# Two layers of linear attention and gated feed-forward on one core: a broadcast through DRAM in longer rows, the feed-forward weights loaded later and in smaller pieces, and a new list of turns

## The chip, the cores and the metric

The kernel runs on one core of a Trainium2 chip. A core has five engines that run their own instruction streams in order and wait for one another by semaphores: TensorE (PE in the profile, with its weight loads as PEld), VectorE (DVE), ScalarE (ACT), GpSimd (POOL) and SyncE (SP). SyncE computes nothing here: it issues transfers (DMA). ScalarE issues some too. The metric is the device time of one execution in microseconds (us); the median of the runs shown is compared.

## The reference

The input x is 2048 rows of 512 numbers in bfloat16. Two kinds of blocks alternate, A B A B, with the same weights both times, so the kernel speaks of two layers of one A and one B each:

```
x = x + A(layernorm(x));  x = x + B(layernorm(x))      # twice

A: q, k, v = x @ wqkv                       # 32 heads of 16
   pq, pk  = q @ w_phi[h], k @ w_phi[h]     # per head, 16x16
   phi(p)  = [softmax(p), softmax(-p)]      # 32 features per head
   kv = sum over rows of phi_k^T v ;  z = sum over rows of phi_k
   out = (phi_q kv) / (phi_q z + 1e-6), heads joined, @ wo
B: h = (x @ W_gate where positive) * (x @ W_up) ;  h @ W_down      # 512 -> 1376 -> 512
```

The attention isn't causal: no query of a layer can be finished before the sums kv and z hold all 2048 keys.

## The kernel before, in words

**Tiles and slabs.** x stays in on-chip memory as 16 tiles of 128 rows (`x_sb`). Most work is done by slabs of 2, 4, 4, 4 and 2 tiles (`SLABS`); in names such as `la04` or `es/12/1` the first digit is the layer (0 or 1) and the second the slab.

**Start.** `load_x` (L732) and `load_w` (L742) bring x and the pieces of wqkv. `fold` multiplies w_phi into the key and query weights: it turns each piece by TensorE (`tr`, L713), copies it out (`evict`, L813 on VectorE, L816 on ScalarE), multiplies by a block-diagonal w_phi and copies the result to `Wkp` or `Wqp`.

**Keys.** For each slab `into_a` runs `layernorm` and then `keys`. `layernorm` takes statistics on VectorE (L840), makes the normalized row tile `ytile` on ScalarE (L882) or VectorE (L885), and turns it to `yA` (for A) or `yG` (for B): for the slabs in `XPOSE` by a transposing DMA that SyncE issues for each tile (L890), else by TensorE (L914) and copies. `keys` multiplies by `Wkp` and `wv` (all such products go through the helper `mm`, so they share L709), takes the two exponentials on ScalarE (L942), sums them by head on VectorE (L948), divides the values by these sums (`vhat`, L962, VectorE or GpSimd) and adds the products with the keys (L974) into `kvsum`.

**Queries.** After the sums of the layer, `out_of_a` takes each slab. `queries` makes the exponentials `expq` (L1043). `attend` multiplies them with the sums (L1071 and around), and from that makes `aT` (L1106): for each row and head the two factors, one for each sign of the exponential, by which `expq` has to be scaled. Head and row lie in `aT` so that they must be spread over 16 partitions each. For slabs 0 and 1 `spread` does that by TensorE (multiplied in at L1195 and L1198). For slabs 2, 3 and 4 it goes through DRAM: SyncE writes `aT` to a scratch (L1116), reads it back with each row repeated 16 times into `abT` (L1120), and `scale` (L1165) multiplies `expq` by it, one of four column groups at a time, on VectorE or GpSimd. Then come the products with `kvbd` (L1132), wo, the residual (L1202) and the normalization for B.

**Feed-forward.** `glu` does a slab's gate and up products, relu on ScalarE (L1254), gate times up on VectorE (`hT`, L1256) and the product with W_down. 1280 of the 1376 columns are in `Wg`, `Wu` and `Wd`, loaded by L761, L762 and L763; a rest of 96 goes another way with weights of its own (`Wl`, `rest`). In layer 0, `glu` of a slab is followed by the keys of layer 1 for that slab.

**Order.** The program is first recorded as a list of operations with what each reads and writes. `schedule()` then puts them in order for every engine with a cost model: among the operations that are ready it goes by `TURNS`, a list with one number for each operation. `ENG` is a table that says on which engine an operation runs or which queue issues a load, where there is a choice (`es/` for the scales, `fc` and `ft` for copies of the folded weights, `vh/` for vhat, `ot/`, `vc/`, `yc/` and `za/` for other copies out, `ld/` for loads, `ms/` for fills). `HOLD` can put operations with a tag behind a given operation on the same queue. `plan()` chooses the semaphores. The result is fixed when the kernel is built; on the chip each engine goes through its own list in order, and an instruction that waits holds up all behind it.

Of the kernel before, what the change touches and what calls it, by code (L numbers as in the profile page):

```python
# [7 lines left out]
BF16 = mybir.dt.bfloat16  # L8
# [4 lines left out]
P = 128  # L13
# [9 lines left out]
HOLD = {}  # L23
ENG = {'ap/a01/0': 'dve',
 'ap/a01/1': 'dve',
# [5 lines left out]
 'ap/a10/0': 'act',  # L31
 'ap/a11/0': 'act',
 'ap/a11/2': 'act',
 'ap/a12/3': 'act',
# [3 lines left out]
 'ap/g02/0': 'act',  # L38
 'ap/g02/1': 'act',
 'ap/g02/3': 'act',  # L40
# [5 lines left out]
 'ap/g12/1': 'act',  # L46
 'ap/g12/2': 'act',
 'ap/g13/2': 'act',
 'ap/g13/3': 'act',
# [6 lines left out]
 'em/11/02': 'act',  # L56
 'em/11/12': 'act',
 'es/02/0': 'pool',
 'es/02/1': 'pool',
 'es/02/3': 'pool',  # L60
 'es/03/3': 'pool',
 'es/04/0': 'pool',
 'es/04/2': 'pool',
 'es/12/1': 'pool',
 'es/13/0': 'pool',
 'es/13/1': 'pool',
 'es/14/0': 'pool',
 'es/14/1': 'pool',
 'es/14/2': 'pool',
 'fck1': 'act',  # L70
 'fck3': 'act',
 'ftk1': 'act',
 'ftk2': 'dve',
 'ftk3': 'act',
 'ftq1': 'dve',
 'ftq2': 'dve',
 'ld/wk1': 'act',
 'ld/wphi': 'sp',
 'ld/wq1': 'act',
 'ld/wq2': 'act',  # L80
 'ld/wv': 'act',
 'ld/x0': 'act',
 'ms/BD': 'pool',
 'ms/ZD 0': 'pool',
 'ms/hl 0': 'pool',
 'ms/kvs 0 1': 'pool',
 'ms/vsb ones': 'pool',
# [3 lines left out]
 'ot/01/1': 'dve',  # L91
 'ot/01/2': 'dve',
 'ot/02/0': 'dve',
 'ot/02/1': 'dve',
 'ot/02/2': 'dve',
 'ot/03/1': 'dve',
 'ot/03/3': 'dve',
 'ot/04/0': 'dve',
 'ot/04/2': 'dve',
 'ot/04/3': 'dve',  # L100
 'ot/10/1': 'act',
 'ot/10/2': 'dve',
 'ot/11/1': 'dve',
 'ot/11/3': 'dve',
 'ot/12/1': 'dve',
 'ot/12/3': 'dve',
 'ot/13/0': 'dve',
 'ot/13/2': 'dve',
 'ot/14/0': 'dve',
 'ot/14/3': 'dve',  # L110
# [11 lines left out]
 'rz/1/12': 'act',  # L122
 'rz/1/13': 'act',
 'rz/1/15': 'act',
 'rz/1/2': 'act',
 'rz/1/3': 'act',
 'rz/1/4': 'act',
 'rz/1/5': 'act',
 'rz/1/6': 'act',
 'rz/1/7': 'act',  # L130
 'rz/1/8': 'act',
 'rz/1/9': 'act',
 'vc/0/10': 'dve',
 'vc/0/2': 'dve',
 'vc/0/4': 'dve',
 'vc/0/5': 'dve',
 'vc/0/7': 'dve',
 'vc/0/8': 'dve',
 'vc/1/1': 'dve',
# [3 lines left out]
 'vc/1/5': 'dve',  # L143
 'vc/1/7': 'dve',
 'vc/1/9': 'dve',
 'vh/0/1/0': 'dve',
 'vh/0/10/1': 'dve',
 'vh/0/12/0': 'dve',
 'vh/0/13/0': 'dve',
 'vh/0/13/1': 'dve',  # L150
 'vh/0/14/1': 'dve',
 'vh/0/15/1': 'dve',
 'vh/0/3/1': 'dve',
 'vh/0/4/0': 'dve',
 'vh/0/4/1': 'dve',
 'vh/0/7/1': 'dve',
 'vh/1/0/1': 'dve',
 'vh/1/11/1': 'dve',
 'vh/1/12/0': 'dve',
 'vh/1/15/0': 'dve',  # L160
 'vh/1/15/1': 'dve',
 'vh/1/2/0': 'dve',
 'vh/1/2/1': 'dve',
 'vh/1/4/0': 'dve',
 'vh/1/4/1': 'dve',
 'vh/1/5/0': 'dve',
 'vh/1/6/0': 'dve',
 'vh/1/6/1': 'dve',
 'vh/1/7/1': 'dve',
 'xp/a10': 'sp',  # L170
 'xp/a14': 'sp',
 'xp/g11': 'sp',
 'yc/a00/1': 'dve',
 'yc/a01/00': 'act',
 'yc/a01/01': 'act',
 'yc/a01/02': 'act',
# [13 lines left out]
 'yc/a14/1': 'dve',  # L190
 'yc/g00/1': 'dve',
# [12 lines left out]
 'za/03': 'dve',  # L204
 'za/11': 'dve',
 'za/12': 'dve',
 'za/14': 'dve'}
# [1166 lines left out]
```

## Time and profile before

| | |
|---|---|
| median of three runs | 388.92 us (388.54 to 389.83) |
| the profiled execution's own time | 390.18 us |
| its span | 388.4 us |
| TensorE, VectorE, ScalarE, GpSimd busy | 97%, 71%, 51%, 17% of the span |
| granted clock of TensorE | 1.00 |
| moved by DMA | 27.96 MB, mean 72 GB/s |
| instruction-fetch packets of queue q8 | 29 of 16 KB |

The span is what the profile of one execution covers; its own time has some 2 us more around it. In a profile, a busy TensorE is not TensorE at its best: matmuls are pipelined, so gaps are read from the starts of successive matmuls. The span, cut by the stages of the work:

| from, to (us) | what runs | TensorE busy of the length |
|---|---|---|
| 0, 13.5 | loads, folding | 9.12 of 13.50 |
| 13.5, 30.9 | first keys, last folding | 16.29 of 17.40 |
| 30.9, 59.5 | keys of layer 0 | 27.68 of 28.60 |
| 59.5, 71.1 | sums, first queries | 10.23 of 11.60 |
| 71.1, 203 | rest of layer 0 A, feed-forward, keys of layer 1 among it | 131.68 of 131.90 |
| 203, 262 | last keys of layer 1 and first slabs of its queries | 58.81 of 59.00 |
| 262, 276 | queries of a later slab, through DRAM | 13.15 of 14.00 |
| 276, 388.4 | rest of layer 1 | 109.03 of 112.40 |

A line of a chain or of an engine's list reads: start, length (us), engine, line of the kernel, what is written and from what, how many instructions in a row. A square bracket at the end names the idle time before it and what ended it.

### The profile page before, as it was taken

How to read it: one execution, taken by the hardware profiler on the slowest of the kernel's cores; microseconds unless marked ns; L12 is line 12 of the kernel's file. 1: busy time of each engine (PE TensorE's matmuls, PEld its weight loads, DVE VectorE, ACT ScalarE, POOL GpSimd, SP SyncE). 2: the span in 40 equal slices, each digit the busy share in tenths (PEclk: the TensorE clock that was granted, in tenths of full speed). 3: DMA queues.
4: the chain of work that ended last, by engine and by line, in shares of the span. 5: the costliest groups of instructions: out<-in, count | busy, mean ns of one | idle time of the engine just before them, and what ended most of it. 6: DMA issues, size and time to landing. Idle time of an engine off the chain costs nothing.

```text
span 388.4 us, 8944 instructions
## 1 busy us (share of the span) xinstructions
PE 376.0 (97%) x3719; PEld 197.8 (51%) x3719; DVE 275.2 (71%) x560; ACT 198.6 (51%) x443; POOL 67.7 (17%) x64
## 2 busy tenths in 40 slices
PE   5999998999999999999999999999999999999996
PEld 2644454384444544444566455475444544454574
DVE  6999987978854887565986996679965556473243
ACT  3999898833542236045416689993263231334021
POOL 4044940051200200200120554001000412000000
PEclk9999999999999999999999999999999999999999
DMA  8995201043450132004004010132444121221002
GB/s 246 286 351 88 42 3 35 31 134 92 111 113 26 47 69 54 2 14 81 2 7 57 3 29 3 32 87 92 119 89 121 42 62 39 58 66 56 0 29 62
DMA packets 57545, 27.96 MB, mean 72 GB/s; under 512 B 39360, under 2 KB 55840, under 8 KB 57504
## 3 DMA queue, kind: packets, MB, share of 16 engines
q1 hardware_dynamic: 55968, 25.98, 27.0%
q10 hardware_dynamic: 1536, 1.41, 1.2%
q8 instruction: 29, 0.48, 0.5%
q14 instruction: 12, 0.10, 0.1%
HBM read 15.25 MB, written 4.00 MB: 50 GB/s over the span
## 4 chain that ended last, share of the span: by engine, by line
PE 81%; DMA 5%; DVE 5%; ACT 5%; SPq 2%; issue 1%; POOL 0%; DVEq 0%
PE pb L709 76%; PE pb L974 2%; DMA abT<-spread 2%; DMA hT<-in_A_wqkv_dram 1%; DVE expq L1198 1%; ACT expk L942 1%; SPq L1120 1%; DMA yA<-ytile 1%; PE pb L1132 1%; DVE expq L1195 1%; DVE x_sb L1202 1%; ACT hT L816 1%; PE pb L1058 1%; DMA spread<-aT 1%; PE pb L1071 1%
## 5 line engine op out<-in xcount | busy, mean ns | idle before, releaser
L709 PE MATMUL pb<-yG,Wu 128*128 128x512 bf16 (+1 forms) x400 | 94.4, 337 | 0.0
L709 PE MATMUL pb<-Wd,hT 128*128 128x512 bf16 (+4 forms) x363 | 94.2, 373 | 0.0
L709 PE MATMUL pb<-yG,Wg 128*128 128x512 bf16 (+1 forms) x400 | 92.8, 337 | 0.3 <-DVE hT L1256 0.2
L1254 ACT ACTIVATE gate_sb<-pb 128x512 bf16<-128x512 f32 x80 | 47.0, 597 | 86.3 <-PE pb L709 55.8
L1256 DVE TENSOR_TENSOR hT<-gate_sb,pb 128x512 bf16<-128x512 bf16 x80 | 54.0, 682 | 44.6 <-PE pb L709 32.3
L962 POOL TENSOR_TENSOR vhat<-vsb,rZk 128x544 bf16<-128x544 bf16 x40 | 43.2, 1102 | 110.3 <-DVE vhat L962 36.8
L1202 DVE TENSOR_TENSOR x_sb<-x_sb,pb 128x512 bf16<-128x512 bf16 x59 | 39.2, 678 | 25.1 <-PE pb L709 24.9
L709 PEld LDWEIGHTS pb<-yG,Wu 128*128 128x128 bf16 x400 | 38.9, 98 | 32.5 <-issue 0.8
L709 PEld LDWEIGHTS pb<-yG,Wg 128*128 128x128 bf16 x400 | 38.7, 98 | 31.2 <-DVE hT L1256 0.7
L709 PEld LDWEIGHTS pb<-Wd,hT 128*128 128x128 bf16 (+1 forms) x363 | 34.8, 98 | 35.9 <-issue 0.7
L1165 POOL TENSOR_TENSOR expq<-expq,abT 128x1024 bf16<-128x1024 bf16 (+1 forms) x12 | 20.5, 1720 | 140.9 <-PE pb L709 84.2
L948 DVE TENSOR_REDUCE Zk<-expk 128x64 f32<-128x1024 bf16 x32 | 38.3, 1208 | 4.4 <-ACT expk L942 4.4
L840 DVE BATCH_NORM_STATS2 stats<-x_sb 128x6 f32<-128x512 bf16 x60 | 39.7, 680 | 1.7 <-DMA x_sb<-in_A_x_dram 1.3
L709 PE MATMUL pb<-wv,yA 128*128 128x512 bf16 x128 | 38.6, 379 | 0.9 <-DMA yA<-ytile 0.9
L942 ACT ACTIVATE expk<-pb 128x512 bf16<-128x512 f32 x64 | 35.6, 611 | 6.1 <-PE pb L709 3.7
L709 PE MATMUL pb<-Wkp,yA 128*128 128x512 bf16 x128 | 38.4, 380 | 0.2 <-ACT Wkp L816 0.2
L1043 ACT ACTIVATE expq<-pb 128x512 bf16<-128x512 f32 x64 | 34.9, 615 | 1.0 <-PE pb L709 0.8
L709 PE MATMUL pb<-wo_sb,oT 128*128 128x512 bf16 x128 | 35.2, 379 | 0.0
L709 PE MATMUL pb<-yA,Wqp 128*128 128x512 bf16 (+1 forms) x160 | 33.7, 337 | 0.1
L1222 ACT ACTIVATE gate_sb<-pb 128x192 bf16<-128x192 f32 x16 | 5.3, 333 | 42.9 <-PE pb L709 42.9
L882 ACT ACTIVATE ytile<-x_sb,nmr,rstd 128x512 bf16<-128x512 bf16 x27 | 21.2, 811 | 4.4 <-DVE nmr L874 4.2
L709 PEld LDWEIGHTS pb<-yA,Wqp 128*128 128x128 bf16 x160 | 14.5, 98 | 12.3 <-issue 1.0
(94 smaller groups left out, 340.0 us busy)
## 6 DMA issues: line engine op xcount, KB each, us to landing
abT<-spread SPq DMA_DIRECT2D x32, 128.0 KB
out_dram<-x_sb SPq DMA_DIRECT2D x15, 128.0 KB, 2.7
x_sb<-in_A_x_dram SPq DMA_DIRECT2D x3, 512.0 KB
Wd<-in_B_W_down_dram SPq DMA_DIRECT2D x1, 1280.0 KB
Wg<-in_B_W_gate_dram SPq DMA_DIRECT2D x1, 1280.0 KB
Wu<-in_B_W_up_dram SPq DMA_DIRECT2D x1, 1280.0 KB
sums_scr<-abT SPq DMA_DIRECT2D x5, 256.0 KB, 2.5
Zs<-sums_scr SPq DMA_DIRECT2D x5, 256.0 KB, 2.7
```

The source lines that it names most:

```text
L709: op("pe", lambda e: e.matmul(view(ps), lhsT, rhs, start=start, stop=stop), reads=reads, writes=[ps], occ=max(25.0, 0.4167 * n + 2.6), lat ...
L840: op("dve", lambda e: e.bn_stats(stats[:, t, :], src()), reads=[res], writes=[R("st", t)], occ=580, lat=680, name=f"bn{t}")
L882: op("act", (lambda t, yb: lambda e: e.activation(ytile[:, yb, :], x_sb[:, t, :], ACT.Identity, bias=nmr[:, t, :], scale=rstd[:, t, :]))(t ...
L942: op("act", (lambda i, s, pk: lambda e: e.activation(expk[:, i, s, :], full(pk), ACT.Exp, scale=1.0 - 2.0 * s))(i, s, pk), reads=[pk], wri ...
L948: op("dve", (lambda i, zb: lambda e: e.tensor_reduce(Zk[:, zb, :], expk[:, i, :, :].rearrange("p s (h f) -> p (s h) f", f=16), AX.X, ALU.a ...
L962: op(eng, (lambda i, s, vb, rz: lambda e: e.tensor_tensor(vhat[:, i, s, :, :], vsb[:, vb, :, :], rZk[:, rz, s * 32:(s + 1) * 32].unsqueeze ...
L974: ins = e.matmul(ps.f32()[32 * i:32 * i + 32, g * 34:g * 34 + 34], expk[:, tiles[j], sg, f0:f0 + 32], vhat[:, tiles[j], sg, 8 * c + 2 * i: ...
L1043: op("act", (lambda c0, s, ps: lambda e: e.activation(eqv(st)[:, c0:c0 + per, s, :], ps.f32()[:, 0:per * n].rearrange("p (c n) -> p c n", ...
L1165: op(eng, lambda e: e.tensor_tensor(part, part, abT[:, c].rearrange("p (s n) -> p s n", s=2)[:, :, 0:n], ALU.mult), reads=Re + [R("abT", c ...
L1202: op("dve", lambda e: e.tensor_tensor(x_sb[:, t, :], x_sb[:, t, :], full(ps), ALU.add), reads=[R("x", t), ps], writes=[R("x", t)], occ=597 ...
L1254: op("act", (lambda gb, pg, k: lambda e: e.activation(gate_sb[:, gb, 0:k], pg.f32()[:, 0:k], ACT.Relu))(gb, pg, k), reads=[pg], writes=[R( ...
L1256: op("dve", (lambda gb, hb, pu, k: lambda e: e.tensor_tensor(hT[:, hb, 0:k], gate_sb[:, gb, 0:k], pu.f32()[:, 0:k], ALU.mult))(gb, hb, pu, k),
```

## The change

1. **Spread through DRAM.** The scratch is laid out with both factors of a row and head side by side, and is written twice over, so that four reads with rows of 2 KB (for slabs of four tiles) take the place of eight reads with rows of 1 KB. `scale` follows the new layout.
2. **Feed-forward weights.** `Wg`, `Wu` and ten of eleven parts of `Wd` are each loaded in two halves of 0.64 MB in place of one piece of 1.28 MB. They have the tag `W`, and `HOLD` puts them behind the last row transpose of the normalizations `la04`, that is of the last slab of layer 0. The products that use them depend on the half that they read.
3. **Order.** The cost model gets `RING`, a bound on how far the issue of a transfer may run ahead of the transfers; `TURNS` is a new list; `ENG` changes in many places. Of the 24 scales, 6 are on GpSimd in place of 12; four copies of folded weights (`fck0`, `fck2`, `fcq0`, `fcq2`) go from ScalarE to VectorE; the start's loads are dealt out anew to the two queues that issue them; the fills of `hl` and of the ones in `vsb` go from GpSimd to VectorE.

What is computed stays the same.

```
-HOLD = {}
+HOLD = {'W': ('la04', -1)}
...
-        scratch = [nc.dram_tensor(f"spread{i}", (64, 512), BF16, kind="Internal").ap() for i in range(2)]
+        scratch = [nc.dram_tensor(f"spread{i}", (65536,), BF16, kind="Internal").ap() for i in range(2)]
...
-            dma(BIG, lambda e: e.dma_start(Wg[:], W_gate.rearrange("(c p) f -> p c f", p=P)[:, :, 0:FM]), writes=[R("Wg")], nbytes=1310720, name="ld Wg")
...
+            prog.tag = "W"
+            for h in range(2):
+                for nm, sbuf, W in (("Wg", Wg, W_gate), ("Wu", Wu, W_up)):
+                    dma(ENG.get(f"ld/{nm}{h}", "sp"), (lambda h, sbuf, W: lambda e: e.dma_start(sbuf[:, 2 * h:2 * h + 2], W.rearrange("(c p) f -> p c f", p=P)[:, 2 * h:2 * h + 2, 0:FM]))(h, sbuf, W),
+                        writes=[R(nm, h)], nbytes=950000, name=f"ld {nm}{h}")
+            for h in range(2):
+                dma(ENG.get(f"ld/Wd{h}", "sp"), (lambda h: lambda e: e.dma_start(Wd[:, 5 * h:5 * h + 5, :], W_down[640 * h:640 * h + 640, :].rearrange("(c p) n -> p c n", p=P)))(h),
+                    writes=[R("Wd", h)], nbytes=950000, name=f"ld Wd{h}")
+            prog.tag = ""
...
-                for s in range(2):
-                    dma("sp", (lambda s: lambda e: e.dma_start(scr[32 * s:32 * s + 32, 0:n].rearrange("r (q w) -> q r w", q=4), aT[:, g, s * w:(s + 1) * w]))(s),
...
+                sv = scr[0:128 * n].rearrange("(r k x) -> r k x", k=2, x=2 * n)
+                for k in range(2):
+                    dma("sp", (lambda k: lambda e: e.dma_start(sv[:, k].rearrange("r (q x) -> q r x", q=4), aT[:, g, 0:2 * w]))(k),
...
                 for c in range(NC):
-                    for s in range(2):
-                        dma("sp", (lambda c, s: lambda e: e.dma_start(abT[:, c, 512 * s:512 * s + n], scr[32 * s + 8 * c:32 * s + 8 * c + 8, 0:n].unsqueeze(1).to_broadcast([8, 16, n])))(c, s),
...
+                    dma("sp", (lambda c: lambda e: e.dma_start(abT[:, c, 0:2 * n], sv[8 * c:8 * c + 8].rearrange("r k x -> (r k) x").unsqueeze(1).to_broadcast([16, 8, 2 * n])))(c),
...
-            op(eng, lambda e: e.tensor_tensor(part, part, abT[:, c].rearrange("p (s n) -> p s n", s=2)[:, :, 0:n], ALU.mult),
+            op(eng, lambda e: e.tensor_tensor(part, part, abT[:, c, 0:2 * n].rearrange("p (q s w) -> p q s w", q=4, s=2), ALU.mult),
...
-                               R_yT(b) + [R("W" + nm)], n, f"{nm}{st}")
+                               R_yT(b) + [R("W" + nm, ic // 2)], n, f"{nm}{st}")
```

The lines of the changed kernel are numbered up to nine higher: L709, L890, L974, L1120, L1132 and L1165 of before are L712, L898, L982, L1128, L1140 and L1173 after.

More of the change, by code (lines that the diff above doesn't have):

```diff
@@ L30 @@
  'ap/a03/3': 'dve',
- 'ap/a10/0': 'act',
- 'ap/a11/0': 'act',
+ 'ap/a10/1': 'act',
+ 'ap/a11/1': 'act',
  'ap/a11/2': 'act',
- 'ap/a12/3': 'act',
+ 'ap/a12/1': 'act',
+ 'ap/a12/2': 'act',
+ 'ap/a13/1': 'act',
+ 'ap/a13/3': 'act',
  'ap/a14/1': 'act',
@@ L37 @@
  'ap/g01/2': 'act',
- 'ap/g02/0': 'act',
  'ap/g02/1': 'act',
- 'ap/g02/3': 'act',
+ 'ap/g02/2': 'act',
+ 'ap/g03/1': 'act',
  'ap/g03/2': 'act',
@@ L45 @@
  'ap/g11/0': 'act',
- 'ap/g12/1': 'act',
- 'ap/g12/2': 'act',
+ 'ap/g11/1': 'act',
+ 'ap/g11/3': 'act',
+ 'ap/g12/3': 'act',
+ 'ap/g13/1': 'act',
  'ap/g13/2': 'act',
- 'ap/g13/3': 'act',
  'ap/g14/0': 'act',
@@ L56 @@
  'em/11/02': 'act',
+ 'em/11/11': 'dve',
  'em/11/12': 'act',
- 'es/02/0': 'pool',
  'es/02/1': 'pool',
[L60 to L68, printed above, removed]
+ 'es/03/1': 'pool',
+ 'es/03/2': 'pool',
+ 'es/13/2': 'pool',
  'es/14/2': 'pool',
+ 'es/14/3': 'pool',
+ 'fck0': 'dve',
  'fck1': 'act',
+ 'fck2': 'dve',
  'fck3': 'act',
+ 'fcq0': 'dve',
+ 'fcq2': 'dve',
+ 'ftk0': 'dve',
  'ftk1': 'act',
- 'ftk2': 'dve',
  'ftk3': 'act',
  'ftq1': 'dve',
- 'ftq2': 'dve',
- 'ld/wk1': 'act',
+ 'ftq3': 'dve',
+ 'ld/wk2': 'sp',
  'ld/wphi': 'sp',
+ 'ld/wq0': 'act',
  'ld/wq1': 'act',
- 'ld/wq2': 'act',
- 'ld/wv': 'act',
+ 'ld/wv': 'sp',
  'ld/x0': 'act',
+ 'ld/x1': 'act',
+ 'ld/x2': 'sp',
+ 'ld/x4': 'sp',
+ 'ld/x8': 'act',
  'ms/BD': 'pool',
  'ms/ZD 0': 'pool',
- 'ms/hl 0': 'pool',
  'ms/kvs 0 1': 'pool',
- 'ms/vsb ones': 'pool',
+ 'ms/kvs eps 0': 'pool',
+ 'ms/kvs eps 1': 'pool',
  'ot/00/0': 'dve',
@@ L90 @@
  'ot/00/3': 'act',
- 'ot/01/1': 'dve',
  'ot/01/2': 'dve',
  'ot/02/0': 'dve',
- 'ot/02/1': 'dve',
- 'ot/02/2': 'dve',
+ 'ot/02/3': 'dve',
  'ot/03/1': 'dve',
  'ot/03/3': 'dve',
- 'ot/04/0': 'dve',
+ 'ot/04/1': 'dve',
  'ot/04/2': 'dve',
  'ot/04/3': 'dve',
+ 'ot/10/0': 'dve',
  'ot/10/1': 'act',
@@ L103 @@
  'ot/11/1': 'dve',
- 'ot/11/3': 'dve',
  'ot/12/1': 'dve',
@@ L107 @@
  'ot/13/0': 'dve',
+ 'ot/13/1': 'dve',
  'ot/13/2': 'dve',
  'ot/14/0': 'dve',
+ 'ot/14/1': 'dve',
+ 'ot/14/2': 'dve',
  'ot/14/3': 'dve',
@@ L132 @@
  'rz/1/9': 'act',
+ 'vc/0/0': 'dve',
  'vc/0/10': 'dve',
- 'vc/0/2': 'dve',
- 'vc/0/4': 'dve',
+ 'vc/0/13': 'dve',
  'vc/0/5': 'dve',
+ 'vc/0/6': 'dve',
  'vc/0/7': 'dve',
- 'vc/0/8': 'dve',
- 'vc/1/1': 'dve',
+ 'vc/1/10': 'dve',
  'vc/1/13': 'dve',
@@ L143 @@
  'vc/1/5': 'dve',
+ 'vc/1/6': 'dve',
  'vc/1/7': 'dve',
- 'vc/1/9': 'dve',
- 'vh/0/1/0': 'dve',
+ 'vc/1/8': 'dve',
  'vh/0/10/1': 'dve',
- 'vh/0/12/0': 'dve',
  'vh/0/13/0': 'dve',
- 'vh/0/13/1': 'dve',
+ 'vh/0/14/0': 'dve',
  'vh/0/14/1': 'dve',
+ 'vh/0/15/0': 'dve',
  'vh/0/15/1': 'dve',
- 'vh/0/3/1': 'dve',
- 'vh/0/4/0': 'dve',
  'vh/0/4/1': 'dve',
- 'vh/0/7/1': 'dve',
+ 'vh/0/6/0': 'dve',
+ 'vh/0/8/0': 'dve',
+ 'vh/0/9/0': 'dve',
  'vh/1/0/1': 'dve',
- 'vh/1/11/1': 'dve',
- 'vh/1/12/0': 'dve',
+ 'vh/1/1/0': 'dve',
+ 'vh/1/1/1': 'dve',
+ 'vh/1/14/1': 'dve',
  'vh/1/15/0': 'dve',
  'vh/1/15/1': 'dve',
- 'vh/1/2/0': 'dve',
- 'vh/1/2/1': 'dve',
+ 'vh/1/3/0': 'dve',
  'vh/1/4/0': 'dve',
  'vh/1/4/1': 'dve',
- 'vh/1/5/0': 'dve',
- 'vh/1/6/0': 'dve',
- 'vh/1/6/1': 'dve',
+ 'vh/1/5/1': 'dve',
+ 'vh/1/7/0': 'dve',
  'vh/1/7/1': 'dve',
+ 'vh/1/8/1': 'dve',
+ 'vh/1/9/0': 'dve',
  'xp/a10': 'sp',
@@ L190 @@
  'yc/a14/1': 'dve',
+ 'yc/g00/0': 'dve',
  'yc/g00/1': 'dve',
@@ L203 @@
  'za/02': 'dve',
- 'za/03': 'dve',
+ 'za/04': 'dve',
  'za/11': 'dve',
- 'za/12': 'dve',
- 'za/14': 'dve'}
+ 'za/12': 'dve'}
 XPOSE = ('a02', 'a03', 'a04', 'a11', 'a12', 'a13', 'g01', 'g02', 'g03', 'g12', 'g13', 'g04', 'g14')
@@ L395 @@
     SWITCH = 95.0
+    RING = 5500.0
     CHUNK, CHUNK0 = 256, 193
@@ L760, in build_kernel @@
         if not TRUNC:
-            dma(BIG, lambda e: e.dma_start(Wg[:], W_gate.rearrange("(c p) f -> p c f", p=P)[:, :, 0:FM]), writes=[R("Wg")], nbytes=1310720, name="ld Wg")
-            dma(BIG, lambda e: e.dma_start(Wu[:], W_up.rearrange("(c p) f -> p c f", p=P)[:, :, 0:FM]), writes=[R("Wu")], nbytes=1310720, name="ld Wu")
-            dma(BIG, lambda e: e.dma_start(Wd[:, 0:10, :], W_down[0:1280, :].rearrange("(c p) n -> p c n", p=P)),
-                writes=[R("Wd")], nbytes=1310720, name="ld Wd a")
+            prog.tag = "W"
[7 more added lines that the diff above has]
+            prog.tag = ""
             for k, W in enumerate((W_gate, W_up)):
@@ L1114, in attend @@
                 scr = scratch[cnt["s"] % 2]
-                for s in range(2):
-                    dma("sp", (lambda s: lambda e: e.dma_start(scr[32 * s:32 * s + 32, 0:n].rearrange("r (q w) -> q r w", q=4), aT[:, g, s * w:(s + 1) * w]))(s),
-                        reads=[R("aT", g)], writes=[R("scr", cnt["s"] % 2, s)], nbytes=110000, name=f"aTo{st}", delay=LATE)
+                sv = scr[0:128 * n].rearrange("(r k x) -> r k x", k=2, x=2 * n)
+                for k in range(2):
+                    dma("sp", (lambda k: lambda e: e.dma_start(sv[:, k].rearrange("r (q x) -> q r x", q=4), aT[:, g, 0:2 * w]))(k),
+                        reads=[R("aT", g)], writes=[R("scr", cnt["s"] % 2, k)], nbytes=250000 * n // 512, name=f"aTo{st}", delay=LATE)
                 for c in range(NC):
-                    for s in range(2):
-                        dma("sp", (lambda c, s: lambda e: e.dma_start(abT[:, c, 512 * s:512 * s + n], scr[32 * s + 8 * c:32 * s + 8 * c + 8, 0:n].unsqueeze(1).to_broadcast([8, 16, n])))(c, s),
-                            reads=[R("scr", cnt["s"] % 2, s)], writes=[R("abT", c, s)], nbytes=150000, name=f"abT{st}", delay=LATE)
+                    dma("sp", (lambda c: lambda e: e.dma_start(abT[:, c, 0:2 * n], sv[8 * c:8 * c + 8].rearrange("r k x -> (r k) x").unsqueeze(1).to_broadcast([16, 8, 2 * n])))(c),
+                        reads=[R("scr", cnt["s"] % 2, k) for k in range(2)], writes=[R("abT", c, s) for s in range(2)], nbytes=310000 * n // 512, name=f"abT{st}", delay=LATE)
                 for c in range(NC):
@@ L1160, in scale @@
             n = 128 * SLABS[st]
-            part = eqv(st)[:, c]
+            part = eqv(st)[:, c].rearrange("p s (q w) -> p q s w", q=4)
             Re = [R("eq", st, c, s, q) for s in range(2) for q in range(4)]
```

12 lines of the change are left out of this document (3 added, 9 removed), and 243 rows, old and new, of the table TURNS.

## The prediction

> **What bounds the kernel now.** First the busy shares and the slices of the page. TensorE is busy 97% of the span at a granted clock of 1.00, and no other engine passes 71%. So time can only come out of the gaps of TensorE or of a chain that fills them; the matmuls are 3719 before and after. Then the windows by stage (start and end, length, and busy time with instruction counts of TensorE, weight loads, VectorE, ScalarE and GpSimd).
>
> ```profile
> PE 376.0 (97%) x3719; PEld 197.8 (51%) x3719; DVE 275.2 (71%) x560; ACT 198.6 (51%) x443; POOL 67.7 (17%) x64
> DMA  8995201043450132004004010132444121221002
> ...
> 13.50:30.90 17.40, 16.29 (x178) 7.92 (x177) 17.40 (x39) 17.37 (x41) 6.33 (x6) 1.00 1.08 301
> 30.90:59.50 28.60, 27.68 (x615) 14.12 (x616) 24.87 (x37) 26.41 (x66) 16.35 (x16) 1.00 0.23 39
> ```
>
> From 13.5 to 30.9 VectorE and ScalarE have no idle time and the transfer engines are full (last two columns: DMA share 1.08, 301 GB/s); from 30.9 to 59.5 the transfers are nearly gone (0.23). The stage up to 59.5, all keys and values of layer 0, is thus held by several things at once. After 71 TensorE runs without a gap over 0.4 us, apart from the one at 274. The chain of waits names the gaps.
>
> ```profile
> 25.84 0.72 ACT ytile L882 x2
> 26.56 4.18 DMA yA<-ytile
> 57.95 0.46 PE pb L974 x56
> 58.40 0.89 issue
> 103.71 3.61 DMA abT<-spread
> 107.41 0.69 DVE expq L1165
> 263.02 2.11 DMA spread<-aT
> 267.07 4.82 DMA abT<-spread
> 274.70 0.61 DVE expq L1165
> ```
>
> Read: the third normalization's row goes out as a transposing transfer at 26.56 and lands only at 30.75, because the weights fill the transfer engines until about 28.5 (elsewhere such a transfer takes 2.4 to 2.5). TensorE then stands still once without waiting for anything ("issue", 0.89), and twice for the chain aT, DRAM, abT, VectorE's scale. TensorE's own list gives the price of each.
>
> ```profile
> 30.88 0.38 PE L709 MATMUL pb<-wv,yA 128*128 128x512 bf16 x1 [0.93 <-DMA yA<-ytile]
> 59.29 0.23 PE L974 MATMUL pb<-vhat,expk 128*32 128x34 bf16 x8 [0.89 <-issue]
> 108.76 0.61 PE L709 MATMUL pb<-yG,Wg 128*128 128x512 bf16 x2 [0.22 <-DVE hT L1256]
> 275.36 0.66 PE L1132 MATMUL pb<-expq,kvbd 32*32 32x512 bf16 x32 [0.85 <-DVE expq L1165]
> ```
>
> Measured from start to start of the matmuls, less their own length, these are 1.1, 1.07, 0.39 and 1.02 us. The third is indirect: VectorE's product for the feed-forward stood behind a scale that waited for abT.
>
> **The base.** The profiled execution took 390.18 us, 1.26 above the median 388.92. The sum is made against 390.18, and 1.26 is taken off at the end. A measurement of this kernel can tell about 0.3% (1.17 us) from no change.
>
> **Weights in six pieces, moved.** Before, SP issues three pieces of 1.28 MB at 9.5 to 17.3; after, six of 0.64 MB behind ten row transposes, of which before issued the last at 47. The order of issues in the built program confirms it. On SP they pass nothing that is needed soon: the next issue is at 63.65, and the six at 0.43 to 1.83 us each (the short and the long weight issue; 5.38 was one stuck behind a full queue) take 3 to 11 us. The bytes, 3.9 MB at the 350 to 400 KB per us seen from 19 to 28, need 10 to 11 us and land at about 58; the first matmul on them is at 78. The cover is 20 us, so being later costs nothing; if they began 20 us later each further us would count in full. What goes: the transposes in the full queue. 4.18 becomes 2.5, and the 1.1 us gap at 30 goes (bounds 0 to 1.1). The start's loads no longer share the engines with weights: by the order of issues, and 0.4 to 0.5 us for one on either queue, the first projection of keys begins at about 11.4 in place of 13.5, and the first transposes at about 15.1 in place of 16.5. TensorE could gain 1.3 there (bounds 0 to 2).
>
> **But VectorE sets the end of this stage.** Up to the last product with the row sums, VectorE has 49.1 us of work from 4.2 on and 2.9 of idle, hence 56.2. The new engine choices give it four copies of folded weights at 0.60 (a row of that shape), 0.10 of small terms, one normalized row less at 0.31, and one product of values less at 0.63: +1.56, hence 50.7. ScalarE loses four such copies (0.49 net of overlap each) and gains 0.70: −1.26. Two fills (0.64 and 1.25 on GpSimd) go to VectorE, whose fills of like size took 0.17 and, for half the larger one, 0.48: at most 1.13, into its 1.1 us of idle between 2.0 and 3.2. If the idle went from 2.9 to none, the stage would end 1.3 earlier; with the work filling in better after an earlier start the last product, which is not VectorE's alone, could follow TensorE, whose three gaps (1.3 + 1.1 + 1.07) allow 3.5. I take −1.5: near VectorE's row, since it was full and gets more. Ends −0.5 and −2.5. The pause at 58.22 to 59.29 is in it: it comes where 256 instructions end and the next block has just been fetched (instruction queue of TensorE: fetched from 56.42 to 57.90). The block before began at 55.52, so asking to going on took 3.77 us, and only 2.69 us of work was left in that block. After, the three blocks here hold 3.88, 4.98 and 3.72 us of work at before's durations, so 3.77 fits but for 0.05.
>
> The Trainium skill, Runtime: NRT & Kernel Launch, Instruction fetch mechanics, says that engines stream code in 16 KiB blocks and that crossing into one costs a transfer's tail, mostly hidden. Here the trace disagrees at 58.22, with 1.07 us. By the rule the pause would have another cause and could stay: 1.07 more on the sum.
>
> **The serial chain 59.5 to 71** (sums, spread by TensorE of the first slab, products) has the same operations and durations, and gaps of 0.4, 0.25, 0.41 and 0.95 in both orders as far as the order shows. 0, ends −0.5 and +0.5.
>
> **The spread.** Per slab the writes stay two, with twice the bytes (32 to 64 KB each); the loads go from eight of 128 KB to four of 256. SP's issue of eight took 5.92 us (265.14 to 271.06); four take 2.3 to 3.0. abT is then whole at 268.5 to 270 in place of 271.9. The doubled writes may take longer than 2.11; nothing shows them, ends 0 and another 2.1. Scales on GpSimd go from 12 to 6: each was 2.12 us there for the 1024 columns against 0.61 to 0.68 on VectorE, and the one at 270.66 stretched VectorE's to 1.42 beside it. In the slab at 262 all four are now VectorE's: 4 × 0.64 = 2.6 us, done by 272.6 against 275.3. So the 1.02 at 274 goes, and the 0.39 at 108. −1.4; ends 0 and −1.6 (with small ones beside). Six more scales on VectorE are 3.9 us of 275, in stages where it has 35 to 50% idle.
>
> **The new order elsewhere.** A new list of turns will have stalls of its own, and many evictions change places between VectorE and ScalarE, which past 71 have a quarter to a half of their time idle to take them. Before has, past 71, about 0.7 us of them beside those two (0.32 at 217 the largest). I take +0.6, one such set more; ends 0 and +2.
>
> Sum: −1.5 + 0 − 1.4 + 0.6 = −2.3. 390.18 − 2.3 = 387.9 profiled, 386.6 for the median. Own range, from the likely halves of those ends: 385.2 to 387.7. Chance 0.46.
>
> **Rivals.**
> *VectorE eats the start* (0.16). Its idle stays near 2.9, so the stage gains only 0.5, and the spread gains only 0.4, since the landing at 274 is replaced by VectorE's own queue: −0.5 − 0.4 + 0.6 = −0.3, median 388.6. For it: 17.40 of 17.40 busy. Against: its work starts earlier in every part.
>
> *Slower: weights beside the code* (0.24). The weights now run at 46 to 58, just where TensorE's blocks are shortest. Let T be the time from asking for a block to going on. Each us over 3.88, 4.98 and 3.72 is a stall. Under full transfers before, a block asked for at 16.54 was fetched from 20.16 and used about 6.1 after the asking; at the thin end of the load it was 4.1. With 6.1 the stalls are 2.2 + 1.1 + 2.4 = 5.7, of which 2.0 fall into the room TensorE had before VectorE's end (3.5 − 1.5); net +3.7, median 390.3. With 7 they are 8.4, median 393.0. From T = 5.6 the gain is gone, from 6.0 the kernel is over 0.3% slower. Against: the fetches themselves took 0.97 and 1.09 us in the full load, against 1.49 without; only the start was late.
>
> The Trainium skill, DMA: Bandwidth & Descriptors, Queues, rings and completion order, has each transfer engine take turns between queues packet by packet. By that a fetch waits a packet and this rival falls, with the sum as forecast. The 0.97 and 1.09 agree; the 3.6 us before one start does not.
>
> *Slower: VectorE stuck on scales* (0.09). With 18 in place of 12 scales on its in-order queue, each of six slabs holds up the feed-forward's product as at 108. At the mean of the two seen, 0.70, that is 4.2 − 1.4 = +2.8 in place of −1.4: −1.5 + 2.8 + 0.6 = +1.9, median 390.8. It needs abT landing later than the turn expects in most slabs; four issues in place of eight speak against it.
>
> *The pause at 58 stays* (0.05), wherever its cause lies: 387.7.
>
> **Numbers.** Faster takes the forecast and part of the last: 0.49. Same takes most of the first rival and part of the last: 0.15. Slower takes the second, the third and a tail of the first: 0.36. The range 384.8 to 391.5 leaves out T above about 6.5 and a better stage than −2.5.
>
> **What would show it.** Right: no wait for yA near 30, first normalization's transposes landing in 2.5, last key product about 1.5 earlier, weights landed before 62, no gap over 0.3 at the products (L1140) of the late slabs. Wrong: gaps marked "issue" between 44 and 60 at block ends (second rival); VectorE's scale (L1173) waiting for abT with TensorE behind its products (third); or a first feed-forward matmul waiting for a weight piece.

## The result

The changed kernel takes 392.71 us (median of five, 392.41 to 393.36), the kernel before beside it 389.07. The ratio is 1.009, with a 95% interval of 1.0068 to 1.0111: about 3.6 us slower, where 2.3 us faster was forecast. It lies above the range, 384.8 to 391.5. The profiled execution took 393.09 with a span of 391.3.

The page's first two views of the changed kernel (52 matmul records are missing from this trace, so TensorE's 95% reads low; its weight loads are complete, and positions in the order are counted by them below):

```profile
PE 371.3 (95%) x3667; PEld 198.3 (51%) x3719; DVE 279.5 (71%) x575; ACT 197.8 (51%) x435; POOL 56.5 (14%) x58
DMA  7803383245432133100100220133636121211002
```

The weights have moved as planned: of the 40 slices of 9.8 us, the third (20 to 29 us) is at 0 where it was at 9 before, and the sixth (49 to 59 us) at 8 where it was at 0. SyncE's own list shows when they are issued:

```profile
27.15 22.08 SPq L898 DMA_TRANSPOSE yA<-ytile  x10
49.27 0.58 SPq L767 DMA_DIRECT2D Wg<-in_B_W_gate_dram  x1
...
51.85 1.34 SPq L770 DMA_DIRECT2D Wd<-in_B_W_down_dram  x2
...
69.09 0.37 SPq L1086 DMA_DIRECT2D sums_scr<-abT  x1
```

The last of the six lands at 63.86 (58 was expected, and 62 named as the latest) and the first product that needs them starts at about 82. No product waits for them, as forecast. What the chain of waits holds in their stead:

```profile
2.78 7.57 DMA hT<-in_A_wqkv_dram
...
14.19 0.69 DVE Wkp L821
...
45.65 4.14 DMA yA<-ytile
...
57.05 1.95 issue
...
63.03 1.08 issue
...
270.65 5.22 DMA abT<-spread
275.89 0.68 DVE expq L1173
...
292.60 3.41 DMA abT<-spread
296.03 0.69 DVE expq L1173
```

TensorE's list, at the same places:

```profile
10.40 0.82 PE L716 MATMUL pb<-ident,hT 128*128 128x128 bf16 x6 [1.55 <-DMA hT<-in_A_wqkv_dram]
...
15.16 1.03 PE L712 MATMUL pb<-Wkp,yA 128*128 128x512 bf16 x4 [0.51 <-DVE Wkp L821]
...
49.93 1.02 PE L712 MATMUL pb<-wv,yA 128*128 128x512 bf16 x4 [0.83 <-DMA yA<-ytile]
...
59.00 0.39 PE L1066 MATMUL pb<-expq,ZO 128*32 128x64 bf16 x28 [1.95 <-issue]
...
64.12 0.48 PE L982 MATMUL pb<-vhat,expk 128*32 128x34 bf16 x41 [1.08 <-issue]
...
277.28 0.65 PE L1140 MATMUL pb<-expq,kvbd 32*32 32x512 bf16 x32 [0.26 <-DVE expq L1173]
...
297.38 0.82 PE L712 MATMUL pb<-yG,Wg 128*128 128x512 bf16 x3 [0.51 <-DVE hT L1264]
```

So the first product with folded key weights starts at 15.16 in place of 13.51, two pauses "issue" of 2.15 and 1.28 from start to start stand where one of 1.07 was, and a row transpose takes 4.14 us again, only later. The same instruction in both traces (start of its weight load, us):

| instruction | before, us | after | difference |
|---|---|---|---|
| first product with folded key weights | 13.50 | 14.94 | +1.4 |
| first product of keys and values | 26.34 | 28.32 | +2.0 |
| last one of layer 0 | 59.31 | 64.39 | +5.1 |
| first product with wo | 71.68 | 74.99 | +3.3 |
| last product of keys and values, layer 1 | 239.24 | 242.59 | +3.3 |
| products of slab 2, layer 1 | 275.35 | 277.28 | +1.9 |
| last product of the kernel | 384.76 | 388.04 | +3.3 |

The loss is made before 65 us; the 1.8 us that come back by 72 are partly work that the new order does earlier (the first sums of the queries come before the last product of layer 0); 1.4 come back at the spread of layer 1, and are lost again behind it.

### The profile page after: what moved, and what is told of

It is laid out like the page before. It is cut to its first block, busy times and chain, and to the rows that moved or that the text cites. A ratio compares the mean times of both kernels' runs of the same rounds, so it can differ in the third digit from the quotient of the medians.

```text
span 391.3 us, 8876 instructions
## 1 busy us (share of the span) xinstructions
PE 371.3 (95%) x3667; PEld 198.3 (51%) x3719; DVE 279.5 (71%) x575; ACT 197.8 (51%) x435; POOL 56.5 (14%) x58
## 3 DMA queue, kind: packets, MB, share of 16 engines
q10 hardware_dynamic: 1392, 1.28, 1.0%
## 4 chain that ended last, share of the span: by engine, by line
PE 75%; DVE 9%; ACT 6%; DMA 6%; issue 2%; SPq 1%; DVEq 0%; ACTq 0%
PE pb L712 70%; DMA abT<-spread 2%; DVE stats L848 2%; DMA hT<-in_A_wqkv_dram 2%; PE pb L982 2%; ACT expq L1051 2%; ACT expk L950 2%; DVE Zk L956 1%; DVE hT L1264 1%; DVE x_sb L1210 1%; DMA yA<-ytile 1%; PE pb L716 1%; ACT ytile L890 1%; DVE oT L821 1%; DMA spread<-aT 1%
## 5 line engine op out<-in xcount | busy, mean ns | idle before, releaser
L712 PE MATMUL pb<-yG,Wg 128*128 128x512 bf16 (+1 forms) x392 | 94.4, 336 | 0.8 <-DVE hT L1264 0.5
L712 PE MATMUL pb<-Wd,hT 128*128 128x512 bf16 (+3 forms) x351 | 93.9, 372 | 0.8 <-DVE nmr L882 0.2
L1262 ACT ACTIVATE gate_sb<-pb 128x512 bf16<-128x512 f32 x80 | 46.7, 596 | 93.6 <-PE pb L712 64.4
L712 PE MATMUL pb<-yG,Wu 128*128 128x512 bf16 (+1 forms) x396 | 91.0, 336 | 0.4
L712 PEld LDWEIGHTS pb<-yG,Wg 128*128 128x128 bf16 x400 | 38.6, 98 | 32.6 <-DVE hT L1264 1.0
L712 PEld LDWEIGHTS pb<-yG,Wu 128*128 128x128 bf16 x400 | 38.9, 98 | 30.4 <-DVE x_sb L1210 0.2
L712 PEld LDWEIGHTS pb<-Wd,hT 128*128 128x128 bf16 (+1 forms) x363 | 34.8, 98 | 37.5 <-issue 0.6
L712 PE MATMUL pb<-wv,yA 128*128 128x512 bf16 x124 | 36.6, 379 | 1.6 <-DMA yA<-ytile 0.8
L712 PE MATMUL pb<-Wkp,yA 128*128 128x512 bf16 x120 | 35.2, 379 | 2.1 <-DVE yA L821 0.8
L712 PE MATMUL pb<-wo_sb,oT 128*128 128x512 bf16 x122 | 33.0, 379 | 0.8 <-issue 0.3
L712 PE MATMUL pb<-yA,Wqp 128*128 128x512 bf16 (+1 forms) x150 | 31.0, 334 | 1.7 <-issue 1.0
L890 ACT ACTIVATE ytile<-x_sb,nmr,rstd 128x512 bf16<-128x512 bf16 x32 | 25.4, 817 | 8.3 <-DVE nmr L882 8.1
L1173 POOL TENSOR_TENSOR expq<-expq,abT 128x1024 bf16<-128x1024 bf16 (+1 forms) x6 | 10.7, 1797 | 123.8 <-PE pb L712 88.6
L712 PEld LDWEIGHTS pb<-yA,Wqp 128*128 128x128 bf16 x160 | 14.3, 98 | 12.1 <-issue 1.0
L712 PEld LDWEIGHTS pb<-wv,yA 128*128 128x128 bf16 x128 | 12.1, 98 | 14.4 <-ACT vsb L824 1.3
```

What stands on the lines that cost most here:

```text
L712: op("pe", lambda e: e.matmul(view(ps), lhsT, rhs, start=start, stop=stop), reads=reads, writes=[ps], occ=max(25.0, 0.4167 * n + 2.6), lat ...
L890: op("act", (lambda t, yb: lambda e: e.activation(ytile[:, yb, :], x_sb[:, t, :], ACT.Identity, bias=nmr[:, t, :], scale=rstd[:, t, :]))(t ...
L1173: op(eng, lambda e: e.tensor_tensor(part, part, abT[:, c, 0:2 * n].rearrange("p (q s w) -> p q s w", q=4, s=2), ALU.mult), reads=Re + [R(" ...
L1262: op("act", (lambda gb, pg, k: lambda e: e.activation(gate_sb[:, gb, 0:k], pg.f32()[:, 0:k], ACT.Relu))(gb, pg, k), reads=[pg], writes=[R( ...
```

## The experiments

All changes of order are made behind the scheduler, so that every engine's list stays as it was but for the transfers named, unless it is said otherwise (experiments 6, 7, 8 and, as it builds on 7, 10). Ratios are to the kernel before, with 95% intervals. Three dots in an edit or a view stand for lines left out.

**1. The changed kernel with the weights early.**

```
         prog.schedule()
+        ref = max(o.start for o in prog.ops if o.name in ("ld Wl", "ld Wd b", "ld wo"))
+        for k, o in enumerate(prog.stages["W"]):
+            o.start = ref + 0.001 * (k + 1)
```

> The changed kernel with its six weight transfers issued right behind the start's last load on SP, ahead of the row transposes; every list else as it was. Theory 1 (the block fetch of TensorE is late while the weights run): the pauses of 2.15 us at 56.9 and 1.25 us at 62.8 become under 0.3 each, the end of layer 0's keys comes about 3 us earlier, and the time falls by 2 to 3.5 us, to about 389.5 to 390.5. Rival (the pauses belong to the order of the instructions, whatever the transfers do): both stay, and the time is within 1 us of 392.7. By the prediction's reading of before, the first transposes should now land about 1.7 us later than the 2.5 us they took.

Measured: 389.13 us, ratio to before 0.9985 (0.9961 to 1.0009). That is 3.6 us under the changed kernel, a little more than expected. Both pauses at 57 and 63 are gone; TensorE's list has no bracket at either block end (56.97 and 60.82):

```profile
56.96 0.42 PE L1066 MATMUL pb<-expq,ZO 128*32 128x64 bf16 x32
...
60.70 0.68 PE L982 MATMUL pb<-vhat,expk 128*32 128x34 bf16 x64
```

The first row transpose, now beside the weights, landed 4.75 us after its issue in place of 2.50, 2.25 later where 1.7 was expected. The place of the weights is thus worth the whole loss, and the rest of the change, with the early weights, comes out even with before.

**2. The kernel before with the weights late**, its three large pieces behind the last row transpose of layer 0.

```
         prog.schedule()
+        ref = prog.stages["la04"][-1].start
+        for k, o in enumerate(o for o in prog.ops if o.name in ("ld Wg", "ld Wu", "ld Wd a")):
+            o.start = ref + 0.001 * (k + 1)
```

> The kernel before with its three large weight transfers moved behind the last row transpose of layer 0, nothing else. Theory 1: one or both of the block ends at 55.5 and 58.2 get a pause of 2 to 5 us in all in place of 1.07, the wait at 29.7 stays as long as a block fetch falls beside the transpose, and the kernel is 1 to 4 us slower than before. Rival (the weights beside the transposes cost the 1.1 us at 29.7 and the fetches cost nothing): that wait goes and the kernel is about 1 us faster.

Measured: 392.40, ratio 1.0081 (1.005 to 1.0112), so 3.0 us slower by this edit alone. The pauses are there, in another order of instructions and with pieces of the old size:

```profile
54.67 0.37 PE L974 MATMUL pb<-vhat,expk 128*32 128x34 bf16 x31
56.08 0.38 PE L974 MATMUL pb<-vhat,expk 128*32 128x34 bf16 x33 [1.04 <-issue]
...
58.25 0.63 PE L974 MATMUL pb<-vhat,expk 128*32 128x34 bf16 x56
61.44 0.23 PE L974 MATMUL pb<-vhat,expk 128*32 128x34 bf16 x8 [2.56 <-issue]
```

The wait for yA at 30, which this experiment's theory 1 let stand, is gone with the early weights: of 1.1 us 0.47 is left there, and for another reason (ScalarE). The prediction was right on that 0.6.

**3. The block ends moved.** In the changed kernel, 64 more instructions on TensorE, at a place where it waits anyway (128 waits, which the trace shows as 64 instructions).

```
...
+            if e == "pe" and o.name == "wcomp" and not self.shifted:
+                self.shifted = True
+                for _ in range(128):
+                    eng.wait_ge(sems["dve"], 1)
             ins = o.fn(eng)
```

> The changed kernel with 64 more instructions on TensorE, waits that have long been met, put where TensorE waits at 5.2 us anyway; nothing else. Every block of 256 instructions now ends 32 matmuls earlier in the order. Theory 1 (the pauses are TensorE waiting for its next block): they move with the count, to matmuls 693 and 821 in the order of the weight loads (before 725 and 852), near 56.0 and 62 us, of about 2.7 and 1.2 us; none at 725 and 852. Rival (they belong to those instructions or to their data): they stay at 725 and 852. The time is within 1.5 us of the changed kernel's either way.

Measured: 394.33, ratio 1.0116 (1.009 to 1.0143), 1.6 us over the changed kernel, where 1.5 at most was expected. The waits themselves cost some of it, since TensorE went on only at 10.66 in place of 7.20; and behind the second pause the granted clock was 0.51 from 64.4 to 67.8 us. The pauses moved with the count: behind weight loads 693 and 821, as expected to the instruction, and nothing at 725 and 852.

```profile
56.91 0.29 PE L1071 MATMUL pb<-expq,ZO 128*32 128x128 bf16 x5
58.41 0.57 PE L1071 MATMUL pb<-expq,ZO 128*32 128x128 bf16 x27 [1.22 <-issue]
...
61.85 0.61 PE L987 MATMUL pb<-vhat,expk 128*32 128x34 bf16 x58
64.83 0.24 PE L987 MATMUL pb<-vhat,expk 128*32 128x34 bf16 x6 [2.36 <-issue]
```

The one pause was expected at 2.7 and came as 1.44 from start to start, the other at 1.2 and came as 2.55; their sum, 4.0, is close to the 3.9 expected. The place of a pause is the block end; what sets the length of each was not shown.

The fetch packets of TensorE's instruction queue, against the ends of the blocks of 256 instructions, tell the rest (us):

| kernel | block end passed | next fetch starts | took | next block end reached | pause there |
|---|---|---|---|---|---|
| before | 55.50 | 56.42 | 1.49 | 58.22 | 1.07 |
| after | 51.50 | 56.52 | 1.08 | 56.85 | 2.15 |
| after | 59.00 | 61.70 | 1.10 | 62.84 | 1.28 |
| 1, weights early | 51.62 | 52.68 | 1.25 | 56.97 | 0 |
| 1, weights early | 56.97 | 57.40 | 1.10 | 60.82 | 0 |
| 2, before, weights late | 47.40 | 53.59 | 1.02 | 54.85 | 1.2 |
| 2, before, weights late | 56.08 | 58.85 | 1.06 | 58.70 | 2.7 |
| 3, block ends moved | 58.41 | 62.26 | 1.10 | 62.27 | 2.55 |
| 5, weights early | 49.55 | 52.36 | 1.42 | 54.90 | 0.3 |
| 5, weights early | 54.90 | 57.07 | 1.34 | 59.06 | 0.8 |

While the weights move, the fetch starts 2.7 to 6.2 us after the block end that it follows. Without them it started 0.4 to 1.1 us after it in experiment 1 and in the first row, but 2.2 and 2.8 us in experiment 5, where no transfer at all was in flight between the two:

```profile
59.86 0.48 PE L982 MATMUL pb<-vhat,expk 128*32 128x34 bf16 x41 [0.60 <-issue]
```

The weights are thus not the only thing that makes a fetch late, and what else does stays open. That they cost is seen in the sum of the pauses at these two block ends: 3.3 to 4.0 us in the four traces with the weights late, none to 1.9 in the ten others. Once begun a fetch takes 1.0 to 1.5 us in every row, and behind a pause of over 1 us TensorE goes on 1.3 to 1.5 us after its end. The time between passing one end and going on beyond the next was 7.5 us for the first pause of the changed kernel, where the block held 5.4 us of work.

**4. The start: key pieces first.** On SyncE, wk1 and wk3 ahead of x tiles 2 to 7; once in the changed kernel and once with the early weights too.

```
...
+        for name, s in zip(("ld wk2", "ld wk1", "ld wphi", "ld wk3", "ld x2", "ld wq3", "ld x4"), slots):
+            next(o for o in sp if o.name == name).start = s
```

> The changed kernel with the pieces of the key weights issued on SP ahead of the x tiles 2 to 7 (wk2, wk1, wphi, wk3, x2, wq3, x4 in place of wk2, x2, wphi, x4, wk1, wk3, wq3). Theory 1 (the start is late because two key pieces stand behind 0.77 MB of x): the last key piece lands near 7.5 in place of 10.9, the first product with the folded key weights comes at about 13 in place of 15.2, and the time falls by 1 to 2 us. Rival (the four copies given to VectorE hold the start): that product stays within 0.5 us of 15.2, and so does the time within 0.5 us.

> Both edits together. If both causes are right and lie one after the other: 3 to 5 us under the changed kernel, 388 to 389.5, no slower than the kernel before. If one engine's total work holds the end of the stage: no more than the larger of the two alone.

Measured: 394.12 (1.012, 1.0089 to 1.0151) and 390.18 (1.0023, 1.0001 to 1.0046): 1.0 to 1.4 us slower than without it, where a gain was expected. The key pieces did land earlier (the last at 8.69 in place of 10.94), but ScalarE's list has the normalization of an x tile ahead of its first copy, and that tile now came later (8.05 in place of 5.34). TensorE's list of the first of the two:

```profile
9.81 0.58 PE L712 MATMUL pb<-hT 128*128 128x128 bf16 x4 [4.27 <-ACT rstd L877]
```

The first product with folded key weights came at 15.57, within the 0.5 us of 15.2 that the rival named, though the time was not. The second expectation's sum falls with it. Neither theory was refuted: the edit had traded one late load for another.

**5. The start again, with one transfer moved:** only x tiles 4 to 7 (0.5 MB) go behind wk1 and wk3; the weights are early.

```
...
+        for name, s in zip(("ld wk1", "ld wk3", "ld x4"), slots):
+            next(o for o in sp if o.name == name).start = s
```

> The changed kernel with the weights early (389.1) and one transfer of the start, the 0.5 MB of x tiles 4 to 7, moved behind the key pieces wk1 and wk3 on SP; x tiles 2 and 3 stay ahead of them, since ScalarE's list has their normalization ahead of the first copy of folded weights. Theory A (the start waits for the key pieces behind x): wk1 lands about 1.5 to 2 us earlier than 10.35, the first product with folded key weights at 13.5 to 14.5 in place of 15.2, time 0.5 to 1.5 us lower. Rival B (the lists wait for the x tiles just as much): that product stays within 0.4 us of 15.2, or the statistics of tiles 4 to 7 hold VectorE and it comes later; time the same or higher.

Measured: 387.39 (386.82 to 387.69), ratio 0.9941 (0.992 to 0.9961): 1.7 us under experiment 1 and faster than the kernel before. Both gains are a little larger than theory A expected. wk1 and wk3 are no longer on the chain; the first product comes at 12.90:

```profile
1.72 4.85 DMA wphi<-in_A_w_phi_dram
6.71 1.05 POOL hT L812
12.15 0.69 DVE Wkp L821
```

```profile
12.90 1.47 PE L712 MATMUL pb<-Wkp,yA 128*128 128x512 bf16 x6 [0.28 <-DVE Wkp L821]
```

So the new start is late because key pieces queue behind x: moving 0.5 MB of it brought the product 2.3 us forward with the copies still on VectorE. Whether those copies cost anything beside is not shown. Part of the 2.3 us is TensorE's own pace: its 128x128 products of the folding start 0.107 us apart up to some moment and 0.056 apart from then on. That moment is 10.8 before, 13.9 in the changed kernel, 14.3 in experiment 1 and 11.0 here, so that 17 more of these products ran at the faster pace here than in experiment 1, about 0.9 us by estimate (17 × 0.051). In this trace the granted clock is 0.50 from 7.6 to 11.0 and 0.99 from 11.0 to 13.0. Part of the gap between two executions here is chance: the small load of w_phi landed between 5.6 and 7.7 in these runs.

**6. The four copies back on ScalarE** (weights early; the four `fc` lines taken out of `ENG`).

> The changed kernel with the weights early and the four copies of folded weights (fck0, fck2, fcq0, fcq2) back on ScalarE, where the kernel before has them; turns as they were. Theory A (those copies on VectorE hold up the start): the first product with the folded key weights comes 0.5 to 1.5 us earlier than 15.4, the end of layer 0's keys 1 to 1.9 us earlier, time 0.5 to 1.5 us under 389.1. Rival B (the start is late because its loads and the statistics of the first tiles are in another order on in-order queues): that product comes within 0.4 us of 15.4 and the time stays within 0.7 us, or rises where ScalarE is the fuller one.

Measured: 397.21 (1.021, 1.0161 to 1.0259); the four executions run from 394.95 to 399.86, and the profile is of the slowest. Not a clean test: the scheduler makes all lists anew when an operation changes engine (386 of 3719 weight loads stand elsewhere), and the same turns then give new waits far from the start (1.4 us at 73 and 1.8 at 94), besides a pause of 1.4 at a block end at 62.3. The first product came at 15.70, 0.5 later than in experiment 1: not the 0.5 to 1.5 earlier of theory A, and just outside the 0.4 of theory B. As the granted clock was 0.50 from 9.4 to 16.2 in this trace, that says little about the copies.

**7. The spread alone, in the kernel before** (the five lines of the diff on `scratch`, writes, reads and `scale`; each pair of old turns of the reads becomes one; the lists are made anew, and 24 of 3719 weight loads and 30 of 560 VectorE instructions come to stand elsewhere).

> The kernel before with the new spread alone: two doubled writes and four reads of 2 KB rows in place of eight reads of 1 KB, turns and engines as they were. By the prediction: abT whole 1.7 to 3.5 us earlier after aT at 263, the waits at 274 (1.02) and 108 (0.39) shrink to under 0.3 each, time 1 to 1.4 us lower. Rival (the reads are limited by the bytes they write, 1 MB on chip a slab in both, and the doubled writes cost what the fewer issues save): abT whole less than 1 us earlier, time within 0.6 us of before.

Measured: 388.53, ratio 0.9975 (0.996 to 0.9991): 0.9 us faster, between the theory's 1 to 1.4 and the rival's 0.6. In layer 1's slab 2 the writes are issued at 262.16 in place of 263.02, and the four reads land at 268.75, 270.20, 271.23 and 272.18. Their last packet ends at 271.54, where before that of the eight reads ends at 274.07: 2.5 us earlier, which is the theory's size. The products no longer wait:

```profile
274.23 0.65 PE L1135 MATMUL pb<-expq,kvbd 32*32 32x512 bf16 x32
...
275.73 0.81 PE L712 MATMUL pb<-wo_sb,oT 128*128 128x512 bf16 x3 [0.42 <-DVE oT L816]
```

The wait of 1.02 is gone, 0.58 returns a step later, for a copy on VectorE. The wait at 108 is under 0.3 as well. The reads land 1.0 to 1.5 us apart here, and in the changed kernel the last three only 0.6 to 0.8 apart; what sets their pace is open.

**8. The old spread, in the changed kernel** (weights early; the same lines back, each turn of a read used for its two).

> The changed kernel with the weights early (389.1 us, w_early) and the old spread put back. If the new spread is worth something with the new order: 0.8 to 1.5 us slower than 389.1, with waits of 1 us or more before the products of layer 1's slab 2. If it is worth nothing: within 0.6 us of 389.1.

Measured: 396.37 (1.0183, 1.0158 to 1.0207), 7 us slower than 389.1, far more than expected. Here the lists are made anew and differ more (464 of 3719 weight loads stand elsewhere), with new waits of 0.8 us at 138, 1.0 at 261, 1.9 at 275 and 0.9 at 298. It suggests that the new turns suit only what they were found for, and gives no price of the spread.

**9. The weights behind the sums, in the kernel before**, where blocks are long.

```
+        ref = min(o.start for o in prog.ops if o.name.startswith("zai"))
+        for k, o in enumerate(o for o in prog.ops if o.name in ("ld Wg", "ld Wu", "ld Wd a")):
+            o.start = ref + 0.001 * (k + 1)
```

> The kernel before with its three large weight transfers moved behind the first read-back of the sums (Zs, at 66.6 us), so that they run from 67 to 78 beside two long blocks of TensorE's instructions. Theory 1 (a fetch is late beside the weights, and costs only where the block is short): no pause at a block end beyond the 1.07 at 58.2; the wait at 29.7 shrinks as it did with the weights at 47 (to 0.47); the first feed-forward matmul at 78.7 waits 0 to 2 us for its weights, and the first slab's abT lands up to 2 us later. Net from 0.6 us faster than before to 1.5 us slower. Rival (weights beside any block cost as much as at 47): 3 us slower.

Measured: 393.93 (1.0116, 1.0077 to 1.0156), 4.5 us slower and outside both expectations; the four executions run from 391.48 to 395.33, and the profile is of the fastest. It has one wait:

```profile
88.31 0.28 PE L709 MATMUL pb<-yG,Wg 128*128 128x256 bf16 x1 [3.45 <-DVE abT L813]
```

Up to there it is 1.1 us ahead of before, with no pause at a block end but 0.6 at 57.5, which is theory 1. The slowdown in this trace is the transfer chain of the next slab, which now stands behind the weights: the writes of `aT` at 73.54 take 5.64 us in place of 2.1. 0 to 2 us were expected for that and it was 3.6. What the slower executions add is not shown.

**10. The third that has room.** The kernel before with the new spread and only W_down behind the sums.

```
...
+        next(o for o in prog.ops if o.name == "ld Wd a").start = ref + 0.001
```

> The kernel before with the new spread (388.5 alone) and the transfer of W_down (1.3 MB) moved behind the read-back of the sums at 66.6, where it has until 87 and no transfer of the chain is due until 74.7. With a third of the early bytes gone the load ends near 25 in place of 28.5, so the block fetch at 26.5 no longer waits for it, and the wait at 29.7 shrinks from 1.1 to about 0.45 as in the two runs that moved all weights. Expected 0.4 to 1.1 us under 388.5; if Wd delays aT's writes or the products of W_down wait for it, 388.5 to 390.

Measured: 388.09, ratio 0.9958 (0.9942 to 0.9974), 0.4 us under experiment 7, the small end of what was expected; the two intervals overlap. Against experiment 7 the wait at 29.7 fell from 1.10 to 0.63 and the pause at 58 from 0.83 to 0.50.

**11. The same on experiment 5.**

> The changed kernel with both cures that worked (weights early; x tiles 4 to 7 behind the key pieces: 387.4) and, as in the run on the kernel before, W_down's two halves moved behind the read-back of the sums. A third less of early bytes lets the fetch asked for at 26.4 begin before 28.9. If that wait still matters here, 0.3 to 0.7 us under 387.4. If not (the wait at 26.6 here is 0.41 us and for a copy of VectorE, not for a transpose), within 0.4 us of 387.4.

Measured: 386.80 (386.22 to 388.46), ratio 0.9945 (0.9925 to 0.9964), against 0.9941: no difference to experiment 5. Both are faster than the two kernels of this case.

## Why the prediction was wrong

**Weights later cost nothing: wrong, and this is the step that failed.** The sum gave the move 0 us; it cost 3.0 to 3.6. The cover named was that of the bytes (put at 58 landed and 78 needed, measured 63.9 and 82), and it held. The cost lay in the rival "weights beside the code", which had the mechanism, the place and the condition, at a chance of 0.24. Its T was put at 6.1 or 7; T was 7.5 and 5.1 in the changed kernel, the pauses 3.4 us against 1.07 before. Its blocks were sized a little off: they held 5.4, 3.8 and 4.7 us of work, not 3.88, 4.98 and 3.72, and the third, begun after the weights had landed, had no pause. Experiments 1 and 2 give the price from both sides, 3.6 and 3.0 us, and experiment 3 shows that it is the block ends. Why the fetch begins late is not shown. The reason given against the rival, that the fetch itself is quick in the full load, was true (1.0 to 1.1) and beside the point: the 3.6 us before its start, seen once before the change, was the term that counted. The Trainium skill, Runtime: NRT & Kernel Launch, Instruction fetch mechanics, calls the cost of crossing into a block mostly hidden; the traces here show 2.7 us at one such crossing. The Trainium skill, DMA: Bandwidth & Descriptors, Queues, rings and completion order, has transfer engines take turns between queues packet by packet. With this the 1.0 to 1.1 us that a fetch took once begun beside the weights agree; the 2.7 to 6.2 us before it began do not.

**The stage's end −1.5: wrong, at its first term.** The start was to gain 1.3 us (bounds 0 to 2) and lost 1.4 to 2.0. The order of issues was read, but not the bytes ahead of each key piece: x tiles 2 to 7, 0.77 MB, went ahead of wk1 and wk3, which then landed at 10.35 and 10.94, where the piece that the kernel before waited for landed at 8.05. Moving 0.5 MB of it behind them gave 1.7 us (experiment 5), a part of it by the earlier step in TensorE's pace. That VectorE would set the stage's end did not show, as the two pauses of TensorE came last there; its added copies were on the chain, but no run put a cost on them.

**The transposes: half right.** Without the weights the wait of 1.1 us at 30 goes to 0.4 to 0.5 (experiments 2 and 9). The first transpose of the changed kernel did land in 2.50, as forecast. But the delay was put down to the full queue alone. In both kernels those that took 4.1 to 4.2 us have a block fetch beside them (at 28.23 before; at 46.73 after, with no weights in flight), and the changed kernel waits 1.21 us for one at 48.7. The full queue delays them as well: with the weights early the first one took 4.75 us (experiment 1) and 5.83 (experiment 5), with the fetch beginning 2.6 and 3.8 us after its issue.

**The serial chain, 0: not so.** By the first product with wo the changed kernel had made up 1.8 us, part of it work moved ahead; no run took that apart.

**The spread −1.4: right in kind.** Alone it gave 0.9 us (experiment 7). The landing was misread: 271.9 is that of the fourth of eight reads, and the last packet of all came at 274.07; nor was `abT` whole at 268.5 to 270, but at 272.18 in experiment 7. In the changed kernel the new spread gave 1.4 at 275, and then the third rival's mechanism appeared once: at 296 VectorE's scale waits for abT, issued between row transposes, and TensorE stands 0.67 us behind the product queued after it.

**New stalls +0.6.** By difference: with both loads put right (experiment 5) the changed kernel is at 387.39, 2.2 us under its own runs of before, of which the spread has 0.9. The new order is then worth about a microsecond of gain, not a loss; this is argued, not measured by itself.

## What to carry to other kernels

A transfer that nothing waits for is not free while an engine with long code runs: count the work in each block of its instructions beside the transfer, and put large loads beside the blocks that last longest, away from dense runs of tiny matmuls. Here a block with 7.5 us of work beside the weights still had a pause of 1.2 (experiment 2), and one with 12.8 had none (experiment 9). When loads are dealt out anew, add up the bytes ahead of each piece that is waited for, and check in which order every in-order list needs them: moving the wrong one trades one wait for another. A list of turns found for one set of operations was no use for pricing a part by taking that part out (experiments 6 and 8); changing the place of transfers alone did give prices.

## What the runs showed of the hardware

A transposing transfer of one row tile lands 2.5 us after its issue (median of 567 whose landing the fourteen traces tell, without a TensorE block fetch begun in its first 2.45 us). With such a fetch the median is 3.8 (106 of them, up to 5.0). With no packet of over 256 bytes from any other transfer in flight it is still 2.5 without a fetch (371, nine in ten under 2.6) and 3.7 with one (72, up to 4.3). So a transpose beside a fetch is late even when no load is in flight: the page's median of 2.5 hides those that TensorE then waits for.
